# Attention units in pairs: the key-value products of two units one behind the other, the first unit's attention products after them

## The chip, the core and the metric

The kernel runs on one core of a Trainium2 chip. A core has TensorE for matmuls (PE in the rows; its weight loads are PEld), the vector engine (DVE), ScalarE (ACT), GpSimd (POOL), and SyncE (SP), which here only issues DMAs. Each engine works through its own queue in order, and semaphores tie the queues together. Matmul results land in PSUM, which has eight banks. The metric is the device time of one execution in microseconds; lower is better.

## What is computed

Linear attention over 8 batches, 8 heads, 576 tokens and 64 channels per head, then two dense layers over the 4608 tokens of 512 channels:

```python
def _attn_ref(q, k, v):
    q_s = np.exp(q - np.max(q, axis=-1, keepdims=True))
    q_s = q_s / (np.sum(q_s, axis=-1, keepdims=True) + 1e-09)
    k_s = np.exp(k - np.max(k, axis=2, keepdims=True))
    k_s = k_s / (np.sum(k_s, axis=2, keepdims=True) + 1e-09)
    kv = np.einsum('bhsd,bhse->bhde', k_s, v)
    return np.einsum('bhsd,bhde->bhse', q_s, kv)

def _moe_ref(x, w_gate, w_val, w_out, rms_g):      # d_ff 1536
    xn = x / np.sqrt(np.mean(x * x, axis=-1, keepdims=True) + 1e-06) * rms_g
    g = xn @ w_gate
    return (g * (1.0 / (1.0 + np.exp(-g))) * (xn @ w_val)) @ w_out

def _moe2_ref(x, w_in, w_out):                     # d_ff 2048
    h = x @ w_in
    return (h * (1.0 / (1.0 + np.exp(-1.702 * h)))) @ w_out
```

The softmax of the keys runs over the tokens, so a 64x64 product of keys and values per head (`kv`) stands between the keys and the queries.

## The kernel before

The first dense layer works on nine tiles of 512 tokens, j = 0 to 8. A tile has 36 slots in twelve rounds of three: part 0 the gate product (`hidden` with w_gate into a bank `ps_gv`), part 1 the value product, part 2 the out product of the round before (`ps_acc`). Each is twelve matmuls of 128x512: products are made of three passes over a high and a low half of the operands. An order written out by hand, `plan[j][slot]`, says what else is issued in a slot, behind its product.

That other work is the attention for the next tile. A unit is a batch and a pair of heads (c = 0 to 3); 32 units, u = 0 to 31. Units 0 to 3 run ahead of the first tile, units 4 to 7 beside tile 0, and from then on four beside each tile up to j = 6. A unit has nine steps (`unit_steps`):

- `s0`: maximum of the keys over the tokens of a partition (DVE, tile m1, L321).
- `s1`: transpose of m1 (PE, L328), maximum (DVE), maximum of the queries and their subtraction (DVE, L335, L336).
- `s2`: transpose of the maximum back (PE, L340) and subtraction from the keys (DVE, L341).
- `s3`: exponentials of keys and queries (ACT, L359, tiles ke and qe), behind a load of ScalarE's table; the DMAs of the next unit's keys, queries and values (`load_kq`, `load_v`, on SP); the sum of the queries' exponentials and the division (DVE, L365 to L368).
- `s4`: the key-value product (PE, L374): ten matmuls, `ke` of 128x64 as the stationary side and the values of 128x65 as the moving one, in turn for the two heads, into the lower and the upper 64 partitions of one bank. Then the read-out by DVE: the sum's reciprocal (L382, L383) and the scaled product in two halves, kvH (L386, two) and kvL (L389, two).
- `qT(0)`, `qT(1)`: five transposes of qe in two groups (PE, L402), copied out as a high half qH (ACT, L410) and a low half qL (DVE, L411).
- `att(0)`, `att(1)`: the attention product of one group, three matmuls (PE, L417 to L419), copied out to xr by ACT (L425). The groups are 256 and 320 tokens wide; which is first alternates with the batch.

Every one of these products takes a bank of the tag `att`, which has two buffers in turn:

```python
    def bank(tag):
        bufs = {"att": 2, "gv": 2, "acc": 4}[tag]
        return ps.tile([P, 512], F32, tag=tag, bufs=bufs, name=f"ps_{tag}")
```

The slots of the steps are in one table, shifted by six slots per unit of a tile:

```python
        AT = (-1, 1, 2, 3, 4, 6, 7, 9, 10)
            order = sorted((AT[s] + 6 * c, c, s) for c in range(len(mine)) for s in range(STEPS))
```

So a unit's key-value product comes in slot 4, behind a value product, its transposes in slots 6 and 7, its attention products in slots 9 and 10. Slot 10 is slot 4 of the next unit: the second attention product of one unit and the key-value product of the next stand side by side there. Behind a unit's last step `squares` adds the square of the finished channel block (ACT, for c > 0 also DVE). At two slots in six a weight of the second layer is decoded (L151 to L157) or stored (L243); after each gate product a high and a low half of an out weight are made (ACT L160, POOL L161). kvH and kvL, like the value tiles, are kept twice, one for even and one for odd units; k_sb, q_sb, ke and qe stand once. qH and qL have two buffers.

Later parts of the kernel, the second dense layer from about 1027 us on, hold no attention.

Of the kernel before, what the change touches and what calls it, by code (L numbers as in the profile page):

```python
# [8 lines left out]
F32 = mybir.dt.float32  # L9
# [11 lines left out]
def attention_glu_mlp(  # L21
# [27 lines left out]
    B, H, S, D = q.shape  # L49
# [3 lines left out]
    P = 128  # L53
# [4 lines left out]
    NC = DM // P  # L58
# [253 lines left out]
    def unit_steps(u, tag="att"):  # L312
        b, c = units[u]
        st = {}
        kH, kL = kvH[u % 2], kvL[u % 2]

        side = nc.gpsimd if u < 2 * NC else nc.vector

        def s0():
            m1 = ap.tile([P, 2, D], F32, tag="m1", bufs=2, name="m1")  # L320
            nc.vector.tensor_reduce(  # L321
                out=m1, in_=kt[u].rearrange("p h r d -> p h d r"), op=ALU.max, axis=AX.X
            )
            st["m1"] = m1

        def s1():
            t = bank(tag)
            nc.tensor.transpose(  # L328
                t[:, 0:P], st["m1"].rearrange("p h d -> p (h d)"), ident
            )  # L330
            m = ap.tile([P, 1], F32, tag="m", bufs=2, name="m")
            nc.vector.reduce_max(out=m, in_=t[:, 0:P], axis=AX.X)
            st["m"] = m
            qm = ap.tile([P, 2, R, 1], F32, tag="qm", bufs=2, name="qm")
            nc.vector.tensor_reduce(out=qm, in_=qt[u], op=ALU.max, axis=AX.X)  # L335
            side.tensor_tensor(qt[u], qt[u], qm.to_broadcast([P, 2, R, D]), op=ALU.subtract)  # L336

        def s2():
            t = bank(tag)
            nc.tensor.transpose(t[:, 0:P], st["m"].to_broadcast([P, P]), ident)  # L340
            nc.vector.tensor_tensor(  # L341
                kt[u],
                kt[u],
                t[:, 0:P]
                .rearrange("p (h o d) -> p h o d", h=2, o=1)
                .to_broadcast([P, 2, R, D]),
                op=ALU.subtract,
            )

        def s3():  # L350
            for n, src in (("k", kt.pop(u)), ("q", qt.pop(u))):
                st[n] = (wp if u < NC else ap).tile(
                    [P, R, 2, D],
                    F32,
                    tag="w" if u < NC else f"{n}e",
                    bufs=NW if u < NC else 1,
                    name=f"{n}e",
                )
                nc.scalar.activation(st[n].rearrange("p r h d -> p h r d"), src, AF.Exp)  # L359
            if NC <= u + 1 < len(units):  # L360
                load_kq(u + 1)
                load_v(u + 1)
            qe = st["q"]
            qs = ap.tile([P, R, 2, 1], F32, tag="qs", bufs=2, name="qs")
            nc.vector.tensor_reduce(out=qs, in_=qe, op=ALU.add, axis=AX.X)  # L365
            nc.vector.tensor_scalar_add(qs, qs, EPS_SUM)
            nc.vector.reciprocal(out=qs, in_=qs)
            side.tensor_tensor(qe, qe, qs.to_broadcast([P, R, 2, D]), op=ALU.mult)  # L368

        def s4():  # L370
            t = bank(tag)
            for r in range(R):
                for h in range(2):
                    nc.tensor.matmul(  # L374
                        t[h * D : (h + 1) * D, 0:VW],
                        st["k"][:, r, h],
                        vt[u][:, h, r, :],
                        start=(r == 0),
                        stop=(r == R - 1),
                    )  # L380
            rs = ap.tile([P, 1], F32, tag="rs", bufs=2, name="rs")
            nc.vector.tensor_scalar_add(rs, t[:, D : D + 1], EPS_SUM)  # L382
            nc.vector.reciprocal(out=rs, in_=rs)  # L383
            for h in range(2):
                a = slice(h * D, (h + 1) * D)
                nc.vector.tensor_scalar_mul(kH[a, a], t[a, 0:D], rs[a])  # L386
            for h in range(2):
                a = slice(h * D, (h + 1) * D)
                nc.vector.scalar_tensor_tensor(  # L389
                    out=kL[a, a],  # L390
                    in0=t[a, 0:D],
                    scalar=rs[a],
                    in1=f(kH[a, a]),
                    op0=ALU.mult,
                    op1=ALU.subtract,
                )

        def qT(i):
            t = bank(tag)
            width = 0  # L400
            for r in halves_of(b)[i]:
                nc.tensor.transpose(  # L402
                    t[:, width : width + P],
                    st["q"][:, r].rearrange("p h d -> p (h d)"),
                    ident,
                )
                width += size(r)
            hi = ap.tile([P, HALF * P + REST], F32R, tag="qH", bufs=2, name="qH")[:, :width]
            lo = ap.tile([P, HALF * P + REST], F32R, tag="qL", bufs=2, name="qL")[:, :width]
            nc.scalar.activation(hi, t[:, :width], AF.Copy)  # L410
            nc.vector.tensor_tensor(lo, t[:, :width], f(hi), op=ALU.subtract)  # L411
            st["q", i] = hi, lo, width

        def att(i):
            hi, lo, width = st["q", i]
            t = bank(tag)
            nc.tensor.matmul(t[:, :width], kH, hi, start=True, stop=False)  # L417
            nc.tensor.matmul(t[:, :width], kH, lo, start=False, stop=False)  # L418
            nc.tensor.matmul(t[:, :width], kL, hi, start=False, stop=True)  # L419
            g0 = b * S + (sum(map(size, halves_of(b)[0])) if i else 0)  # L420
            done = 0
            while done < width:
                j, o = divmod(g0 + done, T)
                n = min(width - done, T - o)
                nc.scalar.activation(xraw(j, c)[:, o : o + n], t[:, done : done + n], AF.Copy)  # L425
                done += n

        return [
            s0, s1, s2, s3, s4,
            lambda: qT(0), lambda: qT(1), lambda: att(0), lambda: att(1),  # L430
        ]
# [375 lines left out]
    with tc.manual_schedule():  # L807
# [49 lines left out]
            plan[j][slot].append(lambda: fn(*args))  # L857

        AT = (-1, 1, 2, 3, 4, 6, 7, 9, 10)

        for j in range(NTILE):
            mine = [(j + 1) * NC + c for c in range(NC) if (j + 1) * NC + c < len(units)]
            for c, u in enumerate(mine):
                steps[u] = unit_steps(u)
            order = sorted((AT[s] + 6 * c, c, s) for c in range(len(mine)) for s in range(STEPS))
            for slot, c, s in order:
                if slot < 0 and j:
                    put(j - 1, SLOTS + slot, steps[mine[c]][s])
# [2 lines left out]
            if j + 1 < NTILE:  # L871
                squares, total, spread, scale = norm_steps(j + 1)
                for c in range(NC):
                    put(j, AT[-1] + 6 * c, squares, c)
                put(j, 30, total)
                put(j, 32, spread)
                for c in range(NC):
                    put(j, 33, scale, c)
# [279 lines left out]
```

## Time and profile before

| what | value |
|---|---|
| median of 3 runs | 1748.82 us (1748.68 to 1748.89) |
| the profiled execution's own time | 1749.04 us |
| its span, first to last instruction | 1747.2 us |
| TensorE busy | 1710.0 us (98%) |
| vector engine busy | 1168.1 us (67%) |
| ScalarE busy | 778.8 us (45%) |
| granted TensorE clock, mean | 0.996 |

The times in the rows are microseconds from the first instruction. A busy share is a mean over the whole span. A timeline row merges equal instructions that follow each other: its first number is the start of the first, its second the time to the end of the last, the count stands at the end. Matmuls are pipelined, so that the next starts before the last has ended; how long one holds TensorE's stream is read from start to start.

### The profile page before, as it was taken

What the parts mean: (1) busy time and instruction counts of PE and PEld (TensorE: products, weight loads), DVE (VectorE), ACT (ScalarE), POOL (GpSimd) and SP (SyncE); (2) the same over time, 40 slices, a digit from 0 to 9 for tenths busy, and PEclk for the clock granted to TensorE, in tenths of its full rate; (3) what the DMA queues carried; (4) which work ended last, traced back from release to release, by engine and by line L of the source; (5) the groups of instructions that cost most, each with busy time, mean ns of one, the idle gap of its engine ahead of it and who ended that gap; (6) DMA issues with size and microseconds to landing.
All of it is one profiled execution on the core that took longest, in us unless ns stands there. A gap on an engine that the chain in (4) does not pass through costs nothing.

```text
span 1747.2 us, 26428 instructions
## 1 busy us (share of the span) xinstructions
PE 1710.0 (98%) x9974; PEld 1508.3 (86%) x9974; DVE 1168.1 (67%) x1955; ACT 778.8 (45%) x1297; POOL 378.9 (22%) x352
## 2 busy tenths in 40 slices
PE   4999999999999999999999999999999999999998
PEld 3666788888888888888888889999999999999998
DVE  7998767667676676765234367555556887777786
ACT  4775444544444444544222345445445533333332
POOL 4875222221222222211112523110003400000000
PEclk9999999999999999999999999999999999999999
DMA  5564332323322233110001134553445564434432
GB/s 163 167 189 134 101 96 81 87 65 101 96 81 78 74 102 95 57 47 1 25 1 49 60 110 157 181 178 137 145 145 167 197 204 133 133 123 131 133 122 85
DMA packets 207631, 193.62 MB, mean 111 GB/s; under 512 B 58896, under 2 KB 188944, under 8 KB 207504
## 3 DMA queue, kind: packets, MB, share of 16 engines
q1 hardware_dynamic: 197376, 174.11, 32.2%
q10 hardware_dynamic: 10128, 17.83, 2.8%
q8 instruction: 78, 1.28, 0.3%
q14 instruction: 49, 0.40, 0.1%
HBM read 123.21 MB, written 68.68 MB: 110 GB/s over the span
## 4 chain that ended last, share of the span: by engine, by line
PE 88%; DVE 6%; ACT 2%; DMA 1%; SPq 1%; issue 1%; POOL 1%; DVEq 0%; ACTq 0%; POOLq 0%
PE ps_gv L527 30%; PE ps_in L709 20%; PE ps_out L1070 19%; PE ps_acc L527 13%; PE ps_acc L557 2%; DVE xr L504 1%; PE ps_att L374 1%; DVE sqa L492 1%; PE ps_att L402 1%; DMA w2oq<-w2od 1%; SPq L271 0%; DVE w L154 0%; PE ps_att L417 0%; DMA stage<-in_moe_w_gate_dram 0%; PE ps_att L418 0%
## 5 line engine op out<-in xcount | busy, mean ns | idle before, releaser
L709 PE MATMUL ps_in<-xf,w2i 128*128 128x384 f32 x2016 | 350.1, 336 | 0.8 <-DVE ev L578 0.8
L709 PEld LDWEIGHTS ps_in<-xf,w2i 128*128 128x128 f32 x2016 | 349.5, 188 | 1.4 <-DVE ev L578 1.2
L527 PE MATMUL ps_gv<-xs,wg 128*128 128x512 f32 x1296 | 321.9, 397 | 2.1 <-ACT xs L518 1.5
L527 PE MATMUL ps_gv<-xs,wv 128*128 128x512 f32 x1296 | 318.2, 394 | 1.5 <-POOL wv L161 1.3
L527 PEld LDWEIGHTS ps_gv<-xs,wg 128*128 128x128 f32 x1296 | 241.9, 189 | 60.8 <-DVE xs L519 3.2
L527 PEld LDWEIGHTS ps_gv<-xs,wv 128*128 128x128 f32 x1296 | 239.1, 188 | 52.6 <-POOL wv L161 3.6
L527 PE MATMUL ps_acc<-u,wo 128*128 128x512 f32 x1152 | 283.5, 395 | 0.0
L1070 PE MATMUL ps_out<-w2o,uf 128*128 128x256 f32 x2268 | 272.9, 282 | 2.0 <-DVE uf L792 2.0
L1070 PEld LDWEIGHTS ps_out<-w2o,uf 128*128 128x128 f32 x2268 | 270.8, 189 | 3.2 <-DVE uf L792 2.4
L527 PEld LDWEIGHTS ps_acc<-u,wo 128*128 128x128 f32 x1152 | 211.9, 188 | 44.3
L905 ACT ACTIVATE s<-ps_gv 128x512 f32<-128x512 f32 x108 | 64.7, 599 | 380.7 <-PE ps_gv L527 380.7
L161 POOL TENSOR_TENSOR wo<-raw,wo 128x512 fp32r<-128x512 f32 x96 | 126.8, 1320 | 490.9 <-ACT wo L160 405.2
L911 DVE TENSOR_TENSOR s<-s,ps_gv 128x512 f32<-128x512 f32 x108 | 73.4, 680 | 178.2 <-PE ps_gv L527 168.0
L694 ACT ACTIVATE h<-h 128x384 f32<-128x384 f32 x144 | 74.2, 525 | 114.0 <-DVE h L733 90.0
L157 POOL TENSOR_TENSOR w<-w,stage 128x512 int32<-128x512 int32 x56 | 76.2, 1361 | 191.9 <-PE ps_gv L527 66.8
L601 DVE TENSOR_TENSOR raw<-raw 128x256 f32<-128x256 f32 (+1 forms) x236 | 107.0, 495 | 9.4 <-DMA raw<-w2d 7.4
L733 DVE TENSOR_TENSOR h<-h,ps_in 128x384 f32<-128x384 f32 x144 | 77.6, 551 | 48.0 <-PE ps_in L709 47.9
L788 ACT ACTIVATE uf<-raw 128x1792 fp32r<-128x1792 f32 x36 | 61.3, 1702 | 85.2 <-PE ps_out L1070 31.5
L1070 PE MATMUL ps_out<-w2oq,uf 128*128 128x256 f32 x756 | 91.6, 282 | 1.3 <-DMA w2oq<-w2od 1.3
L1070 PEld LDWEIGHTS ps_out<-w2oq,uf 128*128 128x128 f32 x756 | 90.5, 189 | 1.5 <-DMA w2oq<-w2od 1.5
L365 DVE TENSOR_REDUCE qs<-qe 128x10 f32<-128x640 f32 x32 | 26.2, 820 | 96.0 <-ACT qe L359 95.9
L792 DVE TENSOR_TENSOR uf<-raw,uf 128x1792 fp32r<-128x1792 f32 x36 | 72.8, 2021 | 19.0 <-ACT uf L788 19.0
(154 smaller groups left out, 1965.2 us busy)
## 6 DMA issues: line engine op xcount, KB each, us to landing
u<-h SPq DMA_DIRECT2D x192, 192.0 KB, 1.9
stage<-in_moe_w_out_dram SPq DMA_DIRECT2D x28, 512.0 KB, 3.6
raw<-u SPq DMA_DIRECT2D x24, 512.0 KB, 4.3
x<-ev ACTq DMA_DIRECT2D x34, 256.0 KB, 2.0
stage<-in_moe_w_in_dram SPq DMA_DIRECT2D x16, 512.0 KB, 3.8
w2d<-w SPq DMA_DIRECT2D x32, 256.0 KB, 2.8
v_sb<-in_v_dram SPq DMA_DIRECT2D x60, 128.0 KB, 3.3
out_dram<-y ACTq DMA_DIRECT2D x29, 256.0 KB, 4.2
```

Source lines behind the costliest of these rows:

```text
L157: return lambda: nc.gpsimd.tensor_tensor(dst, dst, lo, op=ALU.add)
L161: nc.gpsimd.tensor_tensor(dst[:, 1, :], src, f(dst[:, 0, :]), op=ALU.subtract)
L527: nc.tensor.matmul(t, w(a), x(e), start=first and i == 0, stop=last and i == 2)
L601: engine.tensor_tensor(raw[:, o], raw[:, a], raw[:, b], op=op)
L694: nc.scalar.activation(dst, src, AF.Gelu_apprx_sigmoid)
L709: nc.tensor.matmul(t, w[:, a, s, c * P : (c + 1) * P], xfac[i, p, c][:, e, :], start=p in (1, 6, 5) and c == 0 and k == 0, stop=c == 1 and ...
L733: nc.vector.tensor_tensor(v, v, t, op=ALU.add)
L788: nc.scalar.activation(w[:, 0], uraw[k][:, 1:8], AF.Copy)
L792: nc.vector.tensor_tensor(w[:, 1], raw, f(w[:, 0]), op=ALU.subtract)
L905: nc.scalar.activation(s, tg, AF.Silu)
L911: nc.vector.tensor_tensor(s, s, tv, op=ALU.mult)
L1070: nc.tensor.matmul(t[:, i * Q : (i + 1) * Q], u[:, a, LEFT[p] - 1, i * P : (i + 1) * P], w[:, e, m % 2, :], start=m == 0 and i == 0 and n ...
```

## The change

For the tiles from j = 1 on the table of slots becomes one for the even and one for the odd unit of a pair, in a cycle of twelve slots. The even unit's key-value product moves from slot 4 to slot 10, directly ahead of the odd unit's. Its two attention products move from slots 9 and 10 to slot 12, both behind the same gate product. The odd unit's transposes move by one slot, from 12 and 13 to 13 and 14; its attention products stay in slots 15 and 16. The tile ke has two buffers now, since two keys wait for their product, and m1 one. The values of the next even unit are loaded behind the odd unit's key-value product, no longer in its `s3`. `squares` follows the moved last step. Tile 0 keeps the old table.

```diff
-            m1 = ap.tile([P, 2, D], F32, tag="m1", bufs=2, name="m1")
+            m1 = ap.tile([P, 2, D], F32, tag="m1", bufs=1, name="m1")
...
-                    bufs=NW if u < NC else 1,
+                    bufs=NW if u < NC else 2 if n == "k" else 1,
...
                 load_kq(u + 1)
-                load_v(u + 1)
+                if u < 2 * NC or u % 2 == 0:
+                    load_v(u + 1)
...
+            if 2 * NC < u + 1 < len(units) and u % 2:
+                load_v(u + 1)
             rs = ap.tile([P, 1], F32, tag="rs", bufs=2, name="rs")
...
         AT = (-1, 1, 2, 3, 4, 6, 7, 9, 10)
+        PAIR = ((-1, 1, 2, 3, 10, 6, 7, 12, 12), (5, 7, 8, 9, 10, 13, 14, 15, 16))
+
+        def slot_of(j, c, s):
+            return PAIR[c % 2][s] + 12 * (c // 2) if j else AT[s] + 6 * c
...
-            order = sorted((AT[s] + 6 * c, c, s) for c in range(len(mine)) for s in range(STEPS))
+            order = sorted((slot_of(j, c, s), c, s) for c in range(len(mine)) for s in range(STEPS))
...
-                    put(j, AT[-1] + 6 * c, squares, c)
+                    put(j, slot_of(j, c, STEPS - 1), squares, c)
```

What this does to the queues is seen in the first pair of tile j = 2. In the changed kernel the same statements stand three to seven lines further down: L374 is L375 there, L402 is L405, L417 is L420, L389 is L392, L527 is L530. TensorE before, from the gate product of slot 9 to the transposes of slot 12 (`ps_gv` are gate and value products, `ps_acc` out products; kvH_75 belongs to the even unit, v_sb_80 to the odd):

```order
L527 MATMUL ps_gv<-xs,wg_840 128x512 x12
L417 MATMUL ps_att<-qH,kvH_75 128x320
L418 MATMUL ps_att<-qL,kvH_75 128x320
L419 MATMUL ps_att<-qH,kvL_77 128x320
L527 MATMUL ps_gv<-xs,wv_879 128x512 x12
L417 MATMUL ps_att<-qH,kvH_75 128x256
L418 MATMUL ps_att<-qL,kvH_75 128x256
L419 MATMUL ps_att<-qH,kvL_77 128x256
L374 MATMUL ps_att<-v_sb_80,ke 64x65 x10
L527 MATMUL ps_acc<-u,wo 128x512 x12
L527 MATMUL ps_gv<-xs,wg_940 128x512 x12
L402 MATMUL ps_att<-ident,qe 128x128 x3
```

TensorE after, from the value product of slot 10 on:

```order
L530 MATMUL ps_gv<-xs,wv_879 128x512 x12
L375 MATMUL ps_att<-v_sb_79,ke 64x65 x10
L375 MATMUL ps_att<-v_sb_80,ke 64x65 x10
L530 MATMUL ps_acc<-u,wo 128x512 x12
L530 MATMUL ps_gv<-xs,wg_940 128x512 x12
L420 MATMUL ps_att<-qH,kvH_75 128x320
L421 MATMUL ps_att<-qL,kvH_75 128x320
L422 MATMUL ps_att<-qH,kvL_77 128x320
L420 MATMUL ps_att<-qH,kvH_75 128x256
L421 MATMUL ps_att<-qL,kvH_75 128x256
L422 MATMUL ps_att<-qH,kvL_77 128x256
L530 MATMUL ps_gv<-xs,wv_992 128x512 x12
```

The two key-value products follow each other, and both attention products of the even unit come two products later, where the odd unit's transposes stood. The vector engine before, from the gated product of slot 10 to the work of slot 11 (numbers tell buffers apart; ps_att_2949 is the odd unit's bank):

```order
L911 TENSOR_TENSOR s_2900<-s_2900,ps_gv_2926 128x512
L543 CAST u_2940<-s_2900 128x512
L544 TENSOR_TENSOR u_2940<-s_2900,u_2940 128x512
L382 TENSOR_SCALAR rs_2960<-ps_att_2949 128x1
L383 RECIPROCAL rs_2960<-rs_2960 128x1
L386 TENSOR_SCALAR kvH1_76<-ps_att_2949,rs_2960 64x64 x2
L389 SCALAR_TENSOR_TENSOR kvL1_78<-ps_att_2949,rs_2960,kvH1_76 64x64 x2
L321 TENSOR_REDUCE m1_2981<-k_sb_82 128x128
```

The vector engine after, at the same place (ps_att_2917 is the even unit's bank, ps_att_2935 the odd unit's):

```order
L918 TENSOR_TENSOR s_2882<-s_2882,ps_gv_2900 128x512
L546 CAST u_2914<-s_2882 128x512
L547 TENSOR_TENSOR u_2914<-s_2882,u_2914 128x512
L385 TENSOR_SCALAR rs_2928<-ps_att_2917 128x1
L386 RECIPROCAL rs_2928<-rs_2928 128x1
L389 TENSOR_SCALAR kvH0_75<-ps_att_2917,rs_2928 64x64 x2
L392 SCALAR_TENSOR_TENSOR kvL0_77<-ps_att_2917,rs_2928,kvH0_75 64x64 x2
L385 TENSOR_SCALAR rs_2949<-ps_att_2935 128x1
L386 RECIPROCAL rs_2949<-rs_2949 128x1
L389 TENSOR_SCALAR kvH1_76<-ps_att_2935,rs_2949 64x64 x2
L392 SCALAR_TENSOR_TENSOR kvL1_78<-ps_att_2935,rs_2949,kvH1_76 64x64 x2
L321 TENSOR_REDUCE m1_2968<-k_sb_82 128x128
```

Two read-outs stand there instead of one, the even unit's first. ScalarE before, in slot 9 and the beginning of slot 10:

```order
L905 ACTIVATE s<-ps_gv 128x512
L425 ACTIVATE xr<-ps_att 128x320
L359 ACT_TABLE_LOAD
L359 ACTIVATE ke<-k_sb 128x2x5x64
L359 ACTIVATE qe<-q_sb 128x2x5x64
```

ScalarE after, at the same place:

```order
L912 ACTIVATE s<-ps_gv 128x512
L359 ACT_TABLE_LOAD
L359 ACTIVATE ke<-k_sb 128x2x5x64
L359 ACTIVATE qe<-q_sb 128x2x5x64
L160 ACTIVATE wo<-raw_835 128x512
```

The copy of the attention output (xr) has left the place ahead of the exponentials.

## Rows read from the trace of the kernel before

**Rows 1.** The page's first part: busy time, share, instructions.

```profile
PE 1710.0 (98%) x9974; PEld 1508.3 (86%) x9974; DVE 1168.1 (67%) x1955; ACT 778.8 (45%) x1297; POOL 378.9 (22%) x352
```

**Rows 2.** Waits of TensorE, 180 to 850 us: the whole answer.

```profile
engine line waited for: us in total, times, longest us
```

**Rows 3.** Key-value line L374, 180 to 800 us: duration ns minimum/median/maximum, starts, forms.

```profile
L374 PE MATMUL ps_att<-v_sb,ke x480: 219/222/272, 182.1 to 789.0; 128*64 128x65 f32 x160
```

**Rows 4.** Timeline of TensorE, first pair of tile 2: start, us, instruction, count.

```profile
307.28 0.31 PE L417 MATMUL ps_att<-qH,kvH 128*128 128x320 f32 x1
...
307.72 2.93 PE L527 MATMUL ps_gv<-xs,wv 128*128 128x512 f32 x12
310.49 0.28 PE L417 MATMUL ps_att<-qH,kvH 128*128 128x256 f32 x1
...
310.94 0.80 PE L374 MATMUL ps_att<-v_sb,ke 128*64 128x65 f32 x20
311.67 3.02 PE L527 MATMUL ps_acc<-u,wo 128*128 128x512 f32 x12
314.53 2.89 PE L527 MATMUL ps_gv<-xs,wg 128*128 128x512 f32 x12
317.26 0.49 PE L402 MATMUL ps_att<-ident,qe 128*128 128x128 f32 x3
```

**Rows 5.** Timeline of TensorE, end of tile 2, without a key-value stop.

```profile
367.35 0.28 PE L417 MATMUL ps_att<-qH,kvH 128*128 128x256 f32 x1
...
367.71 2.91 PE L527 MATMUL ps_acc<-u,wo 128*128 128x512 f32 x12
370.45 2.88 PE L527 MATMUL ps_gv<-xs,wg 128*128 128x512 f32 x12
```

**Rows 6.** Timeline of ScalarE, slot 9 of the same pair.

```profile
307.48 0.60 ACT L905 ACTIVATE s<-ps_gv 128x512 f32<-128x512 f32 x1 [4.23 <-PE ps_gv L527]
307.97 0.43 ACT L425 ACTIVATE xr<-ps_att 128x320 f32<-128x320 f32 x1
308.42 1.28 ACT L359 ACT_TABLE_LOAD   x1
```

**Rows 7.** Timeline of vector engine and GpSimd, slots 9 to 12; brackets: idle before.

```profile
311.12 0.82 DVE L365 TENSOR_REDUCE qs<-qe 128x10 f32<-128x640 f32 x1 [3.81 <-ACT qe L359]
...
311.68 1.29 POOL L161 TENSOR_TENSOR wo<-raw,wo 128x512 fp32r<-128x512 f32 x1 [2.93 <-ACT wo L160]
...
311.97 1.03 DVE L366 TENSOR_SCALAR qs<-qs 128x10 f32<-128x10 f32 x1
...
314.02 0.68 DVE L911 TENSOR_TENSOR s<-s,ps_gv 128x512 f32<-128x512 f32 x1
...
315.81 0.15 DVE L382 TENSOR_SCALAR rs<-ps_att 128x1 f32<-128x1 f32 x1
...
316.82 0.60 DVE L389 SCALAR_TENSOR_TENSOR kvL<-ps_att,rs,kvH 64x64 fp32r<-64x64 f32 x2
...
318.80 0.49 DVE L411 TENSOR_TENSOR qL<-ps_att,qH 128x320 fp32r<-128x320 f32 x1
```

**Rows 8.** Timeline ahead of the tiles: a read-out and the attention product behind it.

```profile
33.55 0.60 DVE L389 SCALAR_TENSOR_TENSOR kvL<-ps_acc,rs,kvH 64x64 fp32r<-64x64 f32 x2
...
34.29 0.35 PE L417 MATMUL ps_acc<-qH,kvH 128*128 128x256 f32 x1 [0.29 <-DVE kvL L389]
```

**Rows 9.** Timeline of both engines, first pair of tile 1, first width 256.

```profile
207.00 0.60 DVE L389 SCALAR_TENSOR_TENSOR kvL<-ps_att,rs,kvH 64x64 fp32r<-64x64 f32 x2
...
207.45 0.38 PE L402 MATMUL ps_att<-ident,qe 128*128 128x128 f32 x2
```

**Rows 10.** Two stretches: length, busy time (instructions) by engine, granted clock, DMA.

```profile
38.00:48.00 10.00, 7.02 (x21) 5.25 (x22) 6.79 (x11) 5.88 (x12) 5.20 (x5) 0.50 0.31 102
...
1380.00:1395.00 15.00, 13.01 (x107) 12.60 (x106) 12.54 (x21) 7.66 (x7) 0.00 (x0) 1.00 0.69 223
```

## The prediction

> **What bounds the kernel now.** I read the page's busy line first: TensorE works 98% of the span, the vector engine 67% [rows 1]. Then the waits of TensorE from 180 to 850 us, which hold all the units that the change moves: the answer has a heading and no row, so in that stretch TensorE never waits for anyone for a time that the profile lists [rows 2]. There every us of TensorE's queue is a us of the kernel, and every wait that the change puts into it is one too. The vector engine has room on average, but an average says nothing about a wait; its queue has to be followed through one pair of units. Before this change each wait ends early enough, and the question is by how much.
>
> The timeline of TensorE around one unit [rows 4] gives the units of work (I call a place by its slot in a pair's cycle of twelve): gate product of slot 9, the even unit's first attention stop at 307.28, value product at 307.72, second attention stop at 310.49, the odd unit's key-value stop at 310.94, out product at 311.67, gate product of slot 12 at 314.53, the odd unit's transposes at 317.26.
>
> **What the change removes.** A key-value stop has 20 narrow matmuls (the program's ten, each as two records) on 64 columns of the array. From the attention stop at 310.49 to the gate product at 314.53 are 4.04 us with such a stop between [rows 4]; the same stretch at the end of a tile, without one, takes 370.45 - 367.35 = 3.10 us [rows 5]. So one stop costs 0.94 us. Its matmuls flow at (0.80 - 0.22) / 19 = 0.03 us, with 0.22 us the duration of a single one [rows 3, 4], 0.61 us for 20. The remaining 0.33 us is paid on entering and leaving, whatever the number of matmuls; part of it is the out product behind it, 2.86 us instead of 2.74 [rows 4, 5], so 0.12 us is what TensorE loses on taking up its stream again. Two stops in one save 0.33 us per pair. Tiles j = 1 to 6 have four units each, so 12 pairs: 12 x 0.33 = 4.0 us.
>
> The transposes and attention stops are only moved. An attention stop costs 0.44 us at width 320 and 0.36 at 256 wherever it stands [rows 4, 5]: nothing gained or lost. The value loads for the next even unit are issued one slot later, behind a wait for TensorE on SyncE's queue; what stands behind them is the store of a decoded weight, for which nobody on the path waits, and the values are next needed a whole pair later. The second key buffer and the single m1 buffer put no new wait on the path that I can find: m1 is read four slots before it is written again. I cost all of these at nothing; were a load late, TensorE would show it at the key-value pair.
>
> **What it adds.** The attention bank has two buffers in turn. Now the pair's two products fill both, and the two attention products of the even unit, which follow in slot 12, take the same two: the first needs the even unit's bank read out, the second the odd unit's. Both are read out by the vector engine, even unit first, then odd, behind everything else of slots 9 and 10 in its queue. Before, only one such read-out stood there, and the product that needed it came at slot 15.
>
> I work this through for the pair whose rows stand there, with first width 320. *TensorE.* Slot 9's gate product ends at 307.28. The value product takes 2.77 (310.49 - 307.72), the pair of key-value stops 0.94 + 0.61 = 1.55, out product 2.74, gate product 2.73: attention is due at 307.28 + 9.79 = 317.07. *Vector engine.* Its chain starts when ScalarE has the exponential of the odd unit's queries, at 311.12 after 3.81 us idle [rows 7], and runs without a gap to the end of the read-out at 316.82 + 0.60 = 317.42. The chain moves ahead only as far as ScalarE does: the copy of the first attention output no longer stands between the activation that ends at 308.08 and the table load, which began at 308.42 [rows 6], 0.33 us. So the even bank is free at 317.09 and the odd one a read-out later; that takes 317.42 - 315.81 = 1.61 [rows 7], so 318.70. From the end of such a read-out to the matmul behind it passes 34.29 - 34.15 = 0.14 us [rows 8]. So:
> - first attention product: due 317.07, starts 317.23, waits 0.16; with 0.12 for taking up again and its own 0.44 it is done at 317.79;
> - second: due 317.79, its bank comes at 318.84, waits 1.05; with 0.12 and its own 0.36 the value product follows at 319.32.
>
> Undisturbed it would be 317.07 + 0.80 = 317.87. The pair loses 1.45 and saves 0.33: +1.12 us. For a pair with first width 256, TensorE is due at 207.45 - 0.19 (the same shift as 317.26 to 317.07), its vector chain ended at 207.60 [rows 9] and would at 207.27; the same steps give waits of 0.15 and 1.13, a loss of 1.52, net +1.19. Six pairs of each: 6 x 1.12 + 6 x 1.19 = 13.9 us. The chain cannot start early after an earlier stall, since ScalarE's activation of slot 9 hangs on TensorE's own gate product: each pair meets the wait anew.
>
> The profiled execution's 1749.04 us plus 13.9 is 1762.9; it lies 0.22 above the median of the runs, so I predict 1762.7.
>
> **Bounds of the unknown terms.** The restart of 0.12 after a wait is taken from a restart after a key-value stop; at zero, 12 x 0.24 = 2.9 us less (1759.8). If ScalarE's 0.33 does not reach the vector engine, 12 x 0.33 = 4.0 more (1766.7). The one term of the chain that looks odd is a 128x10 addition of 1.03 us, beside a GpSimd product that runs 311.68 to 312.97, where a 128x1 addition takes 0.15 [rows 7]. ScalarE's weight copy and GpSimd's product follow the same exponential as before, so I keep 1.03. Were it to take 0.15, the odd bank is free 0.88 sooner: 1753 or so, worked out below.
>
> **Rivals.**
> *The saving alone, 1744.8.* It needs the odd unit's bank at 317.37 at the latest (due 317.07 + 0.44 for the first attention product, less 0.14), 1.33 us sooner than 318.70. For it speaks the vector engine's 33% of idle time [rows 1]; against it that this idle time lies ahead of the chain (the 3.81 us), not in it. The Trainium skill, TensorEngine Tiling (Array Packing), Tiling Modes, Key Properties, says that a change of tiling mode drains TensorE; the 0.33 us agrees, and by this rule alone the change ends here, with 12 drains less. Chance 6%.
> *A short wait, 1752.1.* The chain is 0.88 shorter because the addition no longer meets GpSimd. First attention product: no wait; second due at 317.51, its bank at 317.96, 0.45 + 0.12 - 0.33 = +0.24 us a pair, +0.31 in the other kind, 3.3 us in all. This is also the border of what a measurement of this kernel can tell from no change, about 0.2% or 3.5 us. 8%, half of it on each side.
> *A second wait behind the first, 1767.7.* In slots 13 and 14 the odd unit's transposes take these banks again, and the second needs the vector engine's split of the first behind the gated product and its split, 315.81 - 314.02 = 1.79 us, plus 0.49 [rows 7]; TensorE has an out product of 2.74 us in between, so about 0.4 us of room. If that room goes and as much again is waited, 12 x 0.42 = 5.0 us more. 6%.
> *The clock falls in the gaps.* In a stretch with waits at the start the granted clock was 0.50 (1.2 GHz) over ten us; in another with 1.99 us of TensorE idle in 15 it stayed at 1.00 (2.4 GHz) [rows 10]. The gaps here add to 1.2 us a pair and are like the latter. Were each followed by ten us at half clock, 12 x 5 = 60 us more, some 1823. The Trainium skill, TensorE: Matmul & The Clock Gate, A second HAM failure mode, tells of small idles between groups that turn through PSUM banks and unsettle the clock; that is this rival. 2%.
> That the pair does not stand together is excluded: the order shows the 20 program matmuls one behind the other in each of the 12 pairs.
> The Trainium skill, Perfetto Trace Analysis, Matmuls, advises that independent groups rotate through different PSUM banks, so that the read-out of one overlaps the matmuls of the next. That speaks against this change, which asks for two banks while both are full; it gives no figure, and the forecast stands on the rows alone.
>
> **How the numbers follow.** The forecast has 78%, inside 1758 to 1767. Faster by over 0.2% is the first rival, 6%. Within 0.2%: half of the short wait and a remainder, 5%. Slower: 89%. The range runs from the short wait's upper part, 1753, to just past the second wait, 1769, and leaves out the two ends.
>
> **What would show it.** Right: in the profile after, the waits of TensorE between 180 and 850 us hold a row of the attention product on the vector engine's last read-out step, some 12 long waits of about 1.1 us and up to 12 short ones, 13 to 16 us in all; the key-value rows still 20 matmuls each but 40 in one piece; a stretch with a pair 0.33 us shorter than two with a stop each; the read-out of the odd unit ending 1.6 us behind that of the even. Wrong: no such row (the chain began earlier than ScalarE lets me think), the addition at 0.2 us, or a second row on the transposes. If the key-value pair cost no less than two stops, the saving was mis-sized, and the time lies 4 us higher.

## The result and the profile after

The changed kernel takes 1767.24 us, median of 4 runs (1767.03 to 1767.98), against 1748.75 us of the kernel before in the same comparison (1747.4 to 1748.89). The ratio is 1.0106, 95% interval 1.0094 to 1.0118: slower, by 18.5 us. The forecast was 1762.7, with a range of 1753 to 1769. Sign and main cause were right; 4.5 us were missing, and they came from a place on which the prediction had put no price. The profiled execution took 1767.23 us, its span 1765.4, at a mean granted clock of 0.996, as before.

TensorE is busy 3.7 us longer than before, 1713.7 instead of 1710.0 [rows 1], while the span grew by 18.2 us (1765.4 against 1747.2), so most of the time went into idle stretches. First part of the page of the kernel after:

```profile
PE 1713.7 (97%) x9974; PEld 1506.1 (85%) x9974; DVE 1167.4 (66%) x1955; ACT 782.6 (44%) x1297; POOL 377.0 (21%) x352
```

Where before the waits of TensorE had no row [rows 2], they now have two. Waits of TensorE from 180 to 870 us, the whole answer (the waiting tile and line, who is waited for, us in total, times, longest):

```profile
engine line waited for: us in total, times, longest us
PE ps_att L420 <- DVE kvL L392: 12.2, 12, 1.1
PE ps_acc L530 <- ACT ev L584: 1.7, 6, 0.3
```

The first row is the predicted one: twelve waits of an attention product on the vector engine's last read-out step, one a pair. The second was not predicted: once in each of six tiles an out product waits for ScalarE's copies out of the banks `acc`.

**Per tile.** The matmul that spreads a tile's squares stands once in each of the tiles 1 to 7, always in the same slot, and so marks the period of a tile. Its row by source line, first the kernel before, then the one after (minimum, median, maximum ns; first and last start):

```profile
L486 PE MATMUL ps_att<-sqH,onesR x7: 398/398/398, 263.3 to 911.0; 128*128 128x512 f32 x7
```

```profile
L489 PE MATMUL ps_att<-sqH,onesR x7: 398/398/398, 266.7 to 930.1; 128*128 128x512 f32 x7
```

From first to last mark pass 647.7 us before and 663.4 after. Between lie the pairs of five tiles, so one tile with two pairs takes 15.7 / 5 = 3.14 us longer. The pairs of tile 1 lie ahead of the first mark, which comes 3.4 us later. That makes 19.1 us in six tiles; 0.9 us come back behind the last mark (836.2 us to the end before, 835.3 after). That part lies behind all the moved units, and in the ten experiments below it takes 834.3 to 836.5 us, so 0.9 us is within what it varies by.

**One pair.** TensorE in the first pair of tile 2, the place of [rows 4] (start, us, instruction, count):

```profile
310.56 2.88 PE L530 MATMUL ps_gv<-xs,wv 128*128 128x512 f32 x12
313.38 1.39 PE L375 MATMUL ps_att<-v_sb,ke 128*64 128x65 f32 x40
314.69 3.02 PE L530 MATMUL ps_acc<-u,wo 128*128 128x512 f32 x12
317.55 2.88 PE L530 MATMUL ps_gv<-xs,wg 128*128 128x512 f32 x12
320.53 0.39 PE L420 MATMUL ps_att<-qH,kvH 128*128 128x320 f32 x1
...
322.19 0.36 PE L420 MATMUL ps_att<-qH,kvH 128*128 128x256 f32 x1 [0.97 <-DVE kvL L392]
...
322.62 0.62 PE L530 MATMUL ps_gv<-xs,wv 128*128 128x512 f32 x2
```

And what it waits for, the vector engine beside GpSimd, the place of [rows 7]:

```profile
314.07 0.82 DVE L366 TENSOR_REDUCE qs<-qe 128x10 f32<-128x640 f32 x1 [3.48 <-ACT qe L359]
...
314.63 1.29 POOL L161 TENSOR_TENSOR wo<-raw,wo 128x512 fp32r<-128x512 f32 x1 [2.61 <-ACT wo L160]
...
314.92 1.03 DVE L367 TENSOR_SCALAR qs<-qs 128x10 f32<-128x10 f32 x1
...
319.79 0.60 DVE L392 SCALAR_TENSOR_TENSOR kvL<-ps_att,rs,kvH 64x64 fp32r<-64x64 f32 x2
320.42 0.16 DVE L385 TENSOR_SCALAR rs<-ps_att 128x1 f32<-128x1 f32 x1
...
321.44 0.60 DVE L392 SCALAR_TENSOR_TENSOR kvL<-ps_att,rs,kvH 64x64 fp32r<-64x64 f32 x2
```

The vector engine starts its chain at 314.07 and runs it through. The even unit's bank is read out at 319.79 + 0.60 = 320.39, and the first attention product begins 0.14 later; the odd unit's is out at 322.04, 1.65 later, and the second begins 0.15 behind that. TensorE would have been ready for the first at 317.55 + 2.73 = 320.28. The value product behind the two starts at 322.62; undisturbed it would be 320.28 + 0.80 = 321.08. The pair of attention products loses 1.54 us here.

**The out product that waits.** TensorE and ScalarE in slot 5 of the same tile, where the tile's own first out product stands:

```profile
295.16 1.52 PE L530 MATMUL ps_acc<-u,wo 128*128 128x512 f32 x6
...
296.34 0.58 ACT L584 ACTIVATE ev<-ps_acc 128x512 f32<-128x512 f32 x1
296.97 1.96 PE L530 MATMUL ps_acc<-u,wo 128*128 128x512 f32 x6 [0.29 <-ACT ev L584]
297.32 0.60 ACT L584 ACTIVATE ev<-ps_acc 128x512 f32<-128x512 f32 x1 [0.40 <-ACT ev L584]
...
298.77 0.40 PE L530 MATMUL ps_gv<-xs,wg 128*128 128x512 f32 x1
```

The same place in the kernel before:

```profile
291.92 0.80 PE L374 MATMUL ps_att<-v_sb,ke 128*64 128x65 f32 x20
...
292.66 3.02 PE L527 MATMUL ps_acc<-u,wo 128*128 128x512 f32 x12
292.92 0.58 ACT L581 ACTIVATE ev<-ps_acc 128x512 f32<-128x512 f32 x1
293.90 0.60 ACT L581 ACTIVATE ev<-ps_acc 128x512 f32<-128x512 f32 x1 [0.40 <-ACT ev L581]
...
295.51 0.84 PE L527 MATMUL ps_gv<-xs,wg 128*128 128x512 f32 x3
```

The out product of slot 5 writes the four banks `acc` one after the other, three matmuls each. The banks c = 2 and 3 still hold the tile before, until ScalarE has copied them out (`store_x2`). Before, the copies ended 0.84 and 1.84 us after the out product had begun; its matmuls for bank 3 start nine matmuls, 9 x 2.74 / 12 = 2.06 us, after it, so bank 3 came free some 0.2 us ahead of need. After, the copies end 1.76 and 2.76 us behind the start. ScalarE's order is the same; it is the out product that has moved ahead, by the 0.92 us of the even unit's key-value stop which stood in slot 4 in front of it. It now takes 298.77 - 295.16 = 3.61 us, where an undisturbed out product takes 2.74 [rows 5], so 0.87 us are lost in each of six tiles, 5.2 us. The wait row lists 1.7 of them, about one of the two holes in each out product.

### The profile page after: what moved, and what is told of

Its sections match the earlier page's. It is cut to its first block, busy times and chain, and to the rows that moved or that the text cites. A ratio compares the mean times of both kernels' runs of the same rounds, so it can differ in the third digit from the quotient of the medians.

```text
span 1765.4 us, 26396 instructions
## 1 busy us (share of the span) xinstructions
PE 1713.7 (97%) x9974; PEld 1506.1 (85%) x9974; DVE 1167.4 (66%) x1955; ACT 782.6 (44%) x1297; POOL 377.0 (21%) x352
## 4 chain that ended last, share of the span: by engine, by line
PE 78%; DVE 12%; ACT 5%; issue 2%; DMA 2%; POOL 1%; SPq 0%; DVEq 0%; ACTq 0%; POOLq 0%
PE ps_gv L530 25%; PE ps_in L712 20%; PE ps_out L1077 19%; PE ps_acc L530 11%; DVE xr L507 1%; ACT L359 1%; PE ps_acc L560 1%; DVE sqa L495 1%; DVE kvL L392 1%; DVE kvH L389 1%; DVE qs L366 1%; ACT qe L359 1%; DVE qs L367 1%; PE ps_att L405 1%; DVE s L918 1%
## 5 line engine op out<-in xcount | busy, mean ns | idle before, releaser
L530 PE MATMUL ps_gv<-xs,wg 128*128 128x512 f32 x1296 | 322.5, 397 | 2.1 <-ACT xs L521 1.5
L530 PE MATMUL ps_gv<-xs,wv 128*128 128x512 f32 x1296 | 316.0, 392 | 2.0 <-POOL wv L161 2.0
L530 PEld LDWEIGHTS ps_gv<-xs,wg 128*128 128x128 f32 x1296 | 241.2, 189 | 59.9 <-DVE xs L522 3.2
L530 PE MATMUL ps_acc<-u,wo 128*128 128x512 f32 x1152 | 285.4, 395 | 1.9 <-ACT ev L584 1.7
L530 PEld LDWEIGHTS ps_gv<-xs,wv 128*128 128x128 f32 x1296 | 240.1, 188 | 52.7 <-POOL wv L161 4.0
L530 PEld LDWEIGHTS ps_acc<-u,wo 128*128 128x128 f32 x1152 | 211.6, 188 | 50.0 <-ACT ev L584 7.1
```

Of the source, the lines that this page charges most:

```text
L530: nc.tensor.matmul(t, w(a), x(e), start=first and i == 0, stop=last and i == 2)
```

## The experiments

Two questions stood open: whether the twelve waits are the whole price of the pairs, and whether the out product waits because the key-value stop of slot 4 is gone. That stop would then have been the cover of ScalarE's copies: time of TensorE in which they could end unnoticed. All kernels compute the whole result; the times of before on the same chips were 1748.5 to 1748.8. "Waits" below are those of TensorE from 180 to 870 us.

**1. The second attention product one slot later.** Its bank is then read out long before.

```diff
-        PAIR = ((-1, 1, 2, 3, 10, 6, 7, 12, 12), (5, 7, 8, 9, 10, 13, 14, 15, 16))
+        PAIR = ((-1, 1, 2, 3, 10, 6, 7, 12, 13), (5, 7, 8, 9, 10, 13, 14, 15, 16))
```

> One number of the new table is changed: the even unit's second attention product moves from slot 12 to slot 13, behind the next value product; the first stays in slot 12. Theory A (the second attention product waits for the odd unit's bank, which the vector engine reads out last): in the trace of the changed kernel the second product's wait with its restart costs 1.15 us a pair; a value product of 2.8 us now lies ahead of it, so that wait goes and 13.8 us come back. The bank that it takes is wanted by the next unit's first transpose right behind, which must wait for ScalarE's copy, some 0.3 us in the first pair of a tile, 2 us in all. Forecast 1755 to 1756, the first product's short wait and the waits of the out product stay. Rival B (the time went into the pair of stops themselves, and TensorE's waits only show where it comes to stand): moving one product by a slot changes nothing, 1767 within 2.

Measured: 1755.96 us (1754.73 to 1756.7), ratio 1.0042 (1.0027 to 1.0057). Waits of this kernel:

```profile
PE ps_acc L530 <- ACT ev L584: 1.8, 6, 0.3
PE ps_att L328 <- ACT xr L428: 1.0, 3, 0.4
```

The row of the attention product is gone, and 11.3 us with it. What stays above the kernel before, 7.4 us, can be read from the starts in its trace. The out product's loss is 5.2. The short first wait, which the list leaves out, is about 0.26 us and 0.08 behind it, 4.1 in twelve pairs. The new wait of a transpose costs 0.37 us in tile 2 and 0.54 in tile 3, more than the list says, some 2.7 in six tiles. Less 4.8 for the saving of the pairs that makes 7.2.

**2. The read-outs first in the vector engine's queue.** In slots 10 and 22 the unit's steps are issued ahead of the gated product.

```diff
+                    if j and slot in (10, 22):
+                        for fn in plan[j][slot]:
+                            fn()
+                        plan[j][slot] = []
                     nc.vector.tensor_tensor(s, s, tv, op=ALU.mult)
```

> TensorE's order stays that of the changed kernel. In slots 10 and 22 the key-value pair and both read-outs are issued ahead of the gated product and its split on the vector engine, which moves the read-outs ahead by the 1.79 us that these three take. Theory A (place of the read-out in the vector engine's queue): both banks come free ahead of the attention products, both waits go, 17.2 us come back, 1750.0, with only the out product's wait left. Rival B (stops themselves): 1767 within 2. Rival C (a wait that goes is replaced: gated product and split come 3.2 us later, so the next value product or out product waits for them): some part of the 17 us is lost again, 1755 to 1765, with a new row of the value or out product on the vector engine.

Measured: 1749.80 us (1748.08 to 1752.18), ratio 1.0008 (0.9999 to 1.0017). Its only wait row:

```profile
PE ps_acc L530 <- ACT ev L584: 1.8, 6, 0.3
```

Vector engine and TensorE in the first pair of tile 2:

```profile
315.56 0.60 DVE L392 SCALAR_TENSOR_TENSOR kvL<-ps_att,rs,kvH 64x64 fp32r<-64x64 f32 x2
...
317.21 0.60 DVE L392 SCALAR_TENSOR_TENSOR kvL<-ps_att,rs,kvH 64x64 fp32r<-64x64 f32 x2
317.82 0.31 PE L420 MATMUL ps_att<-qH,kvH 128*128 128x320 f32 x1
317.84 0.69 DVE L922 TENSOR_TENSOR s<-s,ps_gv 128x512 f32<-128x512 f32 x1
...
318.27 0.28 PE L420 MATMUL ps_att<-qH,kvH 128*128 128x256 f32 x1
```

With the gated product and its split behind the read-outs, both banks are out at 317.81 and the two attention products follow one another at 0.45 us. The instructions are the same, only their order in the queue differs; so the 12.2 us belong to what stood ahead of the read-outs. Now the pairs' saving and the out product's loss nearly cancel: the kernel is level with before.

**3. The copies of banks 2 and 3 one slot earlier,** ahead of the exponentials in ScalarE's queue.

```diff
                     nc.scalar.activation(s, tg, AF.Silu)
+                    if n == 1 and j:
+                        for c in range(2, NC):
+                            store_x2(j - 1, c)
...
-                    if n == 1 and j:
-                        for c in range(2, NC):
-                            store_x2(j - 1, c)
```

> The last two of the four copies of a finished tile out of the out product's banks are issued in slot 3, right behind the gate product's activation, instead of in slot 4 behind the exponentials. Theory A2 (the even unit's key-value stop in slot 4 had been the cover for these copies; with it gone the out product of slot 5 reaches the banks too early): the out product's waits and restarts, 0.86 us a tile in six tiles, go, 5.2 us less, 1762.1, and the attention products' waits stay as they are. Rival D (these waits only take up time that would be waited a slot later anyway): 1767 within 1.

Measured: 1766.01 us (1765.39 to 1767.38), ratio 1.0103 (1.0086 to 1.012). The theory of the missing cover expected 1762 and was missed by 4 us. Waits:

```profile
PE ps_att L420 <- DVE kvL L392: 12.2, 12, 1.1
PE ps_att L405 <- DVE qe L369: 1.4, 6, 0.3
```

TensorE from the gate product of slot 6 of tile 2 on:

```profile
297.34 2.88 PE L530 MATMUL ps_gv<-xs,wg 128*128 128x512 f32 x12
300.47 0.52 PE L405 MATMUL ps_att<-ident,qe 128*128 128x128 f32 x3 [0.24 <-DVE qe L369]
300.97 3.02 PE L530 MATMUL ps_gv<-xs,wv 128*128 128x512 f32 x12
```

The out product no longer waits, as that theory said, but the even unit's transposes in slot 6 now do: they need the queries that the vector engine divides once ScalarE has their exponentials, and the copies have pushed these back. From gate to value product pass 300.97 - 297.34 = 3.63 us, in the changed kernel 301.76 - 298.77 = 2.99: 0.64 us lost, where the list says 0.24. In tile 3 it is 0.75. So some 4 us of the 5.2 come back in six tiles, which is the miss. Six waits went and six came. The time alone would have spoken for the rival, the rows do not; the question went on to experiment 7.

**4. The read-out of the odd unit doubled:** four kvH instructions instead of two, the last two with the same values again.

```diff
-            for h in range(2):
-                a = slice(h * D, (h + 1) * D)
+            for h in range(4 if u >= 2 * NC and u % 2 else 2):
+                a = slice(h % 2 * D, (h % 2 + 1) * D)
                 nc.vector.tensor_scalar_mul(kH[a, a], t[a, 0:D], rs[a])
```

> The odd unit's first half of the read-out (two vector instructions of 64x64, 0.63 us with their gaps) is issued twice, with the same values. Theory A: the odd bank comes free 0.63 us later in each of 12 pairs, the second attention product waits that much longer, 7.6 us more, 1774.8; the first product's wait does not change. Rival B (not the read-out): within 1 us of 1767.2.

Measured: 1785.99 us (1784.61 to 1788.53), ratio 1.0216 (1.0201 to 1.0231), 11 us above what was expected. The waits did as expected, 7.5 us more:

```profile
PE ps_att L420 <- DVE kvL L392: 19.7, 12, 1.7
```

The rest is the clock. Three stretches of this kernel (length, busy time of PE, PEld, DVE, ACT, POOL, granted clock, DMA share, GB/s):

```profile
318.00:324.40 6.40, 4.70 (x23) 3.54 (x22) 5.87 (x19) 1.04 (x2) 0.00 (x0) 1.00 0.39 112
324.40:327.80 3.40, 3.40 (x10) 2.71 (x10) 0.80 (x1) 1.42 (x3) 1.28 (x1) 0.50 0.00 0
327.80:335.00 7.20, 7.20 (x36) 5.87 (x35) 5.78 (x11) 1.96 (x4) 0.00 (x0) 1.00 0.01 2
```

And TensorE across them:

```profile
324.03 0.36 PE L420 MATMUL ps_att<-qH,kvH 128*128 128x256 f32 x1 [1.60 <-DVE kvL L392]
...
324.47 4.50 PE L530 MATMUL ps_gv<-xs,wv 128*128 128x512 f32 x12
328.81 0.49 PE L405 MATMUL ps_att<-ident,qe 128*128 128x128 f32 x3
```

Behind the idle of 1.60 us the granted clock is 0.50, 1.2 GHz instead of 2.4, for 3.4 us, and the value product takes 328.81 - 324.47 = 4.34 us where it takes 2.77 at full clock. Six of the twelve waits are followed by such a stretch; if each costs as much as the one shown, that is 6 x 1.57 = 9.4 us. With the 7.5 of the waits that is 16.9 of the 17.4 us by which the span grew (1782.8 against 1765.4).

**5. Both repairs on the old order:** experiments 2 and 3 together.

> As e6_both_waits_mended, but with the even unit's transposes left in slots 6 and 7. Theory A: the out product's 0.86 us a tile go, but the wait of the transposes for the division that e3_store_early showed, 0.5 us with its restart in six tiles, stands in their place: 1743.8 + 3 = 1746.8, a little below e2_readout_first's 1749.8. Rival (the transposes' wait came of the attention product's, and goes with it): 1744.

Measured: 1748.80 us (1747.59 to 1749.38), ratio 0.9998 (0.9989 to 1.0007), 2 us above what was expected. One row is left, that of the transposes, word for word the one shown in experiment 3. Of the miss 1 us is that wait, which costs the 4 us worked out there instead of the 3 expected; the rest I have not traced.

**6. Both repairs, and the even unit's transposes one slot later,** in 7 and 8 instead of 6 and 7, to get past that wait.

> The read-outs ahead of the gated product (as in e2_readout_first), the two copies out of the out product's banks in slot 3 (as in e3_store_early), and the even unit's transposes one slot later, 7 and 8 in place of 6 and 7, since e3_store_early had them wait for the vector engine's division. Theory A (the pair saves two stops' fixed price, and the waits at the attention product and the out product were all that it cost): no wait is left, 12 x 0.40 us less than the kernel before, with 0.40 a pair as the trace of the changed kernel shows it: 1748.6 - 4.8 = 1743.8. Rival: a third wait takes their place, 1747 or more.

Measured: 1749.59 us (1748.95 to 1750.64), ratio 1.0005 (0.9997 to 1.0014); 1743.8 was expected if no other wait took its place, 1747 or more if one did. One did:

```profile
PE ps_gv L530 <- DVE s L925: 4.4, 6, 0.8
```

Now nothing stands between two products any more, and the value product of slot 7 needs the bank `gv` that the vector engine's gated product has not read yet, since that stands behind the division, the division behind the exponentials, and these behind the copies.

**7. Only the second pair of a tile;** units c = 0 and 1 go back to the old slots, so the stop in slot 4 stands again.

```diff
-            return PAIR[c % 2][s] + 12 * (c // 2) if j else AT[s] + 6 * c
+            return PAIR[c % 2][s] + 12 * (c // 2) if j and c > 1 else AT[s] + 6 * c
```

> Only the second pair of a tile stands in the new table, the first two units of a tile keep their old slots; all else as in the changed kernel. Theory A2 (the even unit's stop in slot 4 of a tile was the cover for the copies out of the out product's banks): with that stop back the out product's waits go (5.2 us in six tiles) and six of the twelve pairs lose and save nothing; six pairs stay, each with 1.41 lost in waits at the attention products and 0.40 saved: 1748.6 + 6 x 1.01 = 1754.7. Rival D (the out product's wait comes of ScalarE's work in general, not of the missing stop): it stays, 1759.9.

Measured: 1755.44 us (1754.63 to 1756.46), ratio 1.0039 (1.0026 to 1.0053). Waits:

```profile
PE ps_att L420 <- DVE kvL L392: 6.1, 6, 1.1
```

With the stop back in slot 4 the out product's wait is gone, although no copy was touched, and the time is what six pairs cost, (1755.44 - 1748.8) / 6 = 1.11 us each. This tells the two theories apart that the time of experiment 3 could not: the stop was the cover.

**8. The odd unit's read-out longer by one instruction** (`range(3 if ...)` in the edit of experiment 4), to have the waits grow without the clock.

> As e4_readout_doubled, with one more read-out instruction (0.31 us) in the odd unit instead of two. Theory A (the wait follows the read-out one to one): 12 x 0.31 = 3.7 us more than the changed kernel, 1770.9, if the granted clock stays at 2.4 GHz through idle stretches of TensorE that are 1.3 us long. e4_readout_doubled, with 1.6 us, showed short stretches at 1.2 GHz in half of its pairs and 18.8 us more where the waits explain 7.6. If the clock falls here too, up to 11 us more than that, 1771 to 1782, and the stretches at 0.50 stand behind the attention product's waits.

Measured: 1771.56 us (1770.58 to 1773.61), ratio 1.0131 (1.0117 to 1.0145): 4.3 us above the changed kernel, 3.5 of them in the waits.

```profile
PE ps_att L420 <- DVE kvL L392: 15.7, 12, 1.4
```

Two stretches that hold ten of the twelve pairs, same columns as in experiment 4:

```profile
300.00:420.00 120.00, 116.83 (x599) 94.51 (x598) 80.50 (x141) 55.41 (x90) 25.39 (x19) 1.00 0.29 86
420.00:840.00 420.00, 407.41 (x2117) 329.86 (x2116) 275.44 (x493) 191.34 (x315) 83.68 (x63) 1.00 0.23 70
```

The clock stays at 1.00 behind waits of up to 1.4 us. An instruction of 0.30 us put into the odd unit's read-out costs 12 x 0.30 = 3.6 us: it stands on the path at full price.

**9. Read-outs first, and the even unit's exponentials one slot later,** its transposes too; the copies stay where they were and now come ahead of them.

```diff
-        PAIR = ((-1, 1, 2, 3, 10, 6, 7, 12, 12), (5, 7, 8, 9, 10, 13, 14, 15, 16))
+        PAIR = ((-1, 1, 2, 4, 10, 7, 8, 12, 12), (5, 7, 8, 9, 10, 13, 14, 15, 16))
```

(and the edit of experiment 2)

> e2_readout_first's order, with the even unit's step of the exponentials in slot 4 behind the gated product and the copies out of the out product's banks, and its transposes in slots 7 and 8. In e6_both_waits_mended the six waits of 0.7 us that were left were the value product's of slot 7 on the gated product of slot 4, which stood on the vector engine behind the division and with it behind ScalarE's exponentials. Theory A (those are the last waits at a tile's start): TensorE waits for nothing from 180 to 870 us and 12 x 0.40 us show, 1744. Rival: the keys of the odd unit, whose load follows the exponentials and is now a slot later, come late and the vector engine holds up a product, 1747 or more.

Measured: **1743.42 us** (1742.99 to 1744.03), ratio 0.9967 (0.9955 to 0.9979), below both kernels. The waits of TensorE have no row. The first pair of tile 2, and the row of the tile marks:

```profile
312.83 2.88 PE L530 MATMUL ps_gv<-xs,wg 128*128 128x512 f32 x12
315.55 0.31 PE L420 MATMUL ps_att<-qH,kvH 128*128 128x320 f32 x1
...
316.35 2.97 PE L530 MATMUL ps_gv<-xs,wv 128*128 128x512 f32 x12
```

```profile
L489 PE MATMUL ps_att<-sqH,onesR x7: 398/398/398, 262.9 to 906.3; 128*128 128x512 f32 x7
```

TensorE's stream is whole: 0.80 us from the first attention product to the value product, as it is undisturbed. From mark to mark pass 643.4 us, 4.3 less than before in ten pairs, 0.43 a pair. That is the saving of the pairs without their waits. It holds one thing more: in slots 7 and 8 the even unit's transposes stand beside a transpose of m1, and TensorE's products are interrupted less often.

**10. Read-outs first, and the copies of banks 2 and 3 on the vector engine** in slot 3, out of ScalarE's way.

```diff
-    def store_x2(j, c):
+    def store_x2(j, c, aside=False):
...
-        if last:
+        if last or aside:
```

(called with `aside` right after the Silu of n == 1, for c = 2 and 3, in place of the old call)

> e2_readout_first's order, with the last two copies out of the out product's banks made by the vector engine in slot 3, in the idle time ahead of its chain, and stored over SyncE's queue. Theory A2 (the out product waits because ScalarE makes these copies behind the exponentials): the wait of 0.86 us a tile goes and ScalarE is not later than before, so that nothing takes its place, 1749.8 - 5.2 = 1744.6. Rival (the copies wait for the store of the first two, whose buffers they take, and hold the vector engine up): waits of the transposes or of the value product on the vector engine, 1747 or more.

Measured: 1744.45 us (1742.73 to 1745.45), ratio 0.9974 (0.9963 to 0.9985), and no wait row either. The tile marks:

```profile
L489 PE MATMUL ps_att<-sqH,onesR x7: 398/398/398, 262.8 to 906.5; 128*128 128x512 f32 x7
```

From mark to mark pass 643.7 us, 4.0 less than before, 0.40 a pair, here with the even unit's transposes in their old slots. A second way out of the same two waits comes to nearly the same gain.

## Why the prediction was right, and where it fell short

**The bank wait** is right in kind, place, number and nearly in size. The prediction's account of the two buffers that fill together and of the odd read-out last in the vector engine's queue shows row by row, and three runs bear it out from three sides: give the product more time (1), give the read-out an earlier place (2), make the read-out longer (8).

**Its size.** The steps gave a loss of 1.45 us in the pair shown, and 1.54 were measured: 0.25 ahead of the first product instead of 0.16; 322.19 - (320.53 + 0.44) = 1.22 ahead of the second, where 1.05 and a restart of 0.12 had been worked out; 0.07 behind it instead of 0.12. The read-out takes 1.65 instead of 1.61. The start of the vector engine's chain was right to the hundredth: 314.07 - 310.56 = 3.51 us behind the value product, as 311.12 - 0.33 - 307.28 has it. The first pair of tile 3, with first width 256, loses 1.62 by the same steps (0.25, 1.29, 0.08), where 1.52 had been worked out. The wait row, forecast at 13 to 16 us, lists 12.2, since the short waits are not in it. That each pair meets the wait anew holds, with twelve waits of at most 1.1 us. Keeping the 128x10 addition at 1.03 was right: it stands again at 1.03 beside GpSimd's product, and with it the short wait falls as a rival. That GpSimd's product is what makes it long was not tried.

**The saving** of 0.33 us a pair was low. From the value product's start to the gate product's are 317.55 - 310.56 = 6.99 us, where 2.77 + 1.55 + 2.74 = 7.06 had been worked out: the pair of stops takes 1.48 us, two stops apart 1.88, so 0.40. This takes 2.77 for the value product, as the forecast did. Experiments 10 and 9, with no wait in the way, need no such step and give 0.40 and 0.43. The net of the pair shown is 1.54 - 0.40 = 1.14 us against the forecast's 1.12, and the tile marks have (3.14 - 0.87) / 2 = 1.14 for the mean of all. That it fits so closely is in part luck: the loss was 0.09 too low and the saving 0.07.

**The step that failed** is the one that cost a moved step at nothing when TensorE's own work is the same. It took the stop out of slot 4 at its full price and asked whom the stop itself had waited for, not who had used its time. The time of the stop in slot 4, 0.92 us ahead of the out product, had carried ScalarE's copies out of the banks of the next out product, with some 0.2 us to spare. Take the stop away and 0.87 us come back as a wait in slot 5, in the first pair of a tile only, since the copies come once in a tile. So 13.9 us forecast, and 6 x 0.87 = 5.2 us on top: 19.1, as the tile marks have it for six tiles; 18.5 in the medians.

**The rivals.** The saving alone did not come, and experiments 9 and 10 show what it needs: both waits gone, 4.4 to 5.4 us below the kernel before. The second wait in slots 13 and 14 did not come: no row names those transposes. The clock did not fall behind the changed kernel's waits of 1.1 us, but it was nearer than its 2% said: with idle of 1.6 to 1.7 us in experiment 4 it halved behind six of the twelve waits. The Trainium skill, TensorE: Matmul & The Clock Gate, A second HAM failure mode, tells, of a bf16 kernel, of clock and throughput lost to small idles of TensorE between groups that turn through PSUM banks; the trace of experiment 4 agrees (1.57 us lost behind the wait shown, six such stretches), those of the changed kernel and of experiment 8 do not, since the same cycling with idles of 1.1 and 1.4 us left the clock at 1.00.

The Trainium skill, Perfetto Trace Analysis, Matmuls, wants groups to turn through different banks so that one's read-out overlaps the next's matmuls. The trace agrees, 12.2 us in twelve waits where both banks are full; but experiment 2 mends it with the same two banks, by the order in the reader's queue alone.

**What stays open:** why in experiment 4 six of the waits and not all bring the lower clock. Their length does not decide it: of the six that did, three were of 1.60 or 1.61 us and three of 1.69, and so were the six that did not.

## What to carry to other kernels

When work is taken off the engine that sets the time, look at the next instruction there and ask when what it needs is ready, engine by engine: the removed time may have been another engine's cover, and then it comes back as a wait. When two groups fill all buffers of a bank before one is read out, put the read-outs at the head of the reading engine's queue, or the next user a slot later, before counting any saving. Follow a repair along the queues too: here mending one wait moved it twice to the next user (the transposes, then the value product), until the order on ScalarE itself was changed.

## What the hardware showed that was not expected

- Two key-value products one behind the other, 40 narrow matmul records, take 1.48 us of TensorE's stream, two apart 1.88. Putting them together saved 0.40 us a pair by the tile marks of experiment 10, and 0.43 in experiment 9.
- Idle of TensorE of 1.1 us (the changed kernel) and 1.4 us (experiment 8) a pair left the granted clock at 1.00; idle of 1.6 to 1.7 us in the same place (experiment 4) was followed in six of twelve cases by 3.4 us at 0.50.
- The list of waits shows less than is lost: 1.7 us where the out products' durations say 5.2, and 0.24 us at the transposes of experiment 3 where the starts say 0.64.
